# A chunk's query tokens by one DMA transpose of 512 rows instead of four of 128, with the projection reading whole rows

## The chip, the core and the metric

The kernel runs on one core of a Trainium2 chip. The metric is device time in microseconds (us): several runs of the kernel before and of the other kernel on the same chip. The record marks the state of each run, fast or slow; all runs that are compared by time here were fast. The profile is of one execution, recorded instruction by instruction. Engines are named as in the profile: PE is TensorE's matmuls, PEld its weight loads, DVE VectorE, ACT ScalarE, POOL GpSimd, and SPq the queue on which SyncE issues DMAs.

## The reference

One block of a Conformer over 2 batches of 4000 tokens with 512 features, in bfloat16. Cut to what matters here:

```python
x1 = x + 0.5 * (silu(ln(x) @ w_ff1_a) @ w_ff1_b)
h = ln(x1)
q, k, v = h @ w_q, h @ w_k, h @ w_v
scores = jnp.einsum('btd,bsd->bts', q, k) * D ** -0.5        # 4000 x 4000 per batch
x2 = x1 + jnp.einsum('bts,bsd->btd', softmax(scores), v) @ w_o
# ... then a convolution module, a second feed-forward part and a LayerNorm
```

## The kernel before

Tokens are worked on in chunks of 508 (four tiles of 127), eight per batch, the last of them with 444. The kernel folds `w_q` and `w_k` into one matrix `M`, so a query projection is `M` applied to the normalised tokens `h`, and the keys are `h` itself. During the first feed-forward part the normalised tokens are written to DRAM (`keysd`); attention fetches them from there, with the features on the partitions, by DMA transposes.

Where a chunk's query tokens land: a slot of 4096 bytes per partition, as four tiles, each with four contraction blocks of 128 tokens. The order in a partition's row is (tile, contraction block, token).

```python
oLT = take(2 * 4096)
self.lnT = [C.view(oLT + s * 4096, 2048).rearrange("p (t c k) -> p t c k", t=TPC, c=DC)
            for s in range(2)]
self.b_lnT = [[C.buf("lnT%d" % s, oLT + s * 4096 + j * 1024, 1024) for j in range(TPC)]
              for s in range(2)]
...
self.sT = C.view(oLT + 6144, 1024)...      # transposed row sums, in the second half of slot 1
```

The fetch, one call for each tile (127 or 111 query tokens, fetched as 128 rows), and the projection of one output block of 128 features:

```python
def fetch_queries(self, b, qc, ti):
    sl = self.query_slot(b, qc)
    src, rd = self.keys_at(b, self.query_at(qc, ti)[0])        # 128 rows of keysd
    self.transpose(self.lnT[sl][:, ti], src, rd, [self.b_lnT[sl][ti]])

def q_group(self, b, qc, dc):
    s, sl = qc % 2, self.query_slot(b, qc)
    ps, b_ps = self.sbank()
    W = width(qc)                                               # 508 or 444
    out = ps[:, 0:W].rearrange("p (t k) -> p t k", t=TPC)
    lo = self.query_at(qc, 0)[1]
    for cc in range(DC):
        self.mm(out, self.M[:, cc, dc * 128:(dc + 1) * 128], self.lnT[sl][:, :, cc, lo:lo + W // TPC],
                cc == 0, cc == DC - 1, [self.b_M] + self.b_lnT[sl], b_ps)
    ...                                                         # ACT or DVE copies ps to qT
```

So each projection matmul reads four pieces of 127 tokens that lie 1024 bytes apart. In attention over chunk g the fetch for chunk g + 1 is asked for at key tiles 7 to 10 of 32, and its four blocks of projection stand at key tiles 14, 16, 18 and 20:

```python
if g + 1 < NCK and g != 1 and 7 <= kt < 7 + TPC:
    self.fetch_queries((g + 1) // TCB, (g + 1) % TCB, kt - 7)
```

All DMAs of this kind go out on SyncE's queue in program order. A scheduler written in the kernel keeps track of buffers and emits a semaphore wait before an instruction where one is needed.

## Time and profile before

| | kernel before |
|---|---|
| time, median of 3 runs | 2034.23 us (2033.78 to 2035.38) |
| span of the profiled run | 2030.5 us |
| PE busy | 2021.3 us |
| granted clock | 0.999 |
| query transposes | 64, to landing 2.7 us |

The busy time of PE is almost the whole span, and the chain of work that ended last is 99% PE: whatever does not lengthen or shorten the row of matmuls is not seen in the time. Matmuls of 508 columns are listed with a mean duration of some 370 ns although the next one starts after some 215 ns: they overlap. For their cost one must look at the distances of their starts, which this document takes from the start times in the trace; the timeline shows them rounded to 10 ns. The lines themselves are shown in the prediction.

### The profile page before, as it was taken

The numbers are of one execution on the slowest core, as the hardware profiler recorded it, in microseconds if no ns is written. First come the engines' busy times: TensorE is split into PE (matmuls) and PEld (weight loads), VectorE is DVE, ScalarE is ACT, GpSimd is POOL, SyncE is SP. The second block draws the span as 40 slices with busy tenths as digits, with TensorE's granted clock in tenths as the row PEclk, the third lists the DMA queues.
The fourth block names the chain that finished last, engine by engine and source line by source line (L and its number), as shares of the span: only waits on it lengthen the run. The fifth ranks groups of instructions, "written<-read, shape, count | busy, mean of one in ns | idle before, by whom it ended". The sixth has DMA issues, their size and how long they took to land.

```text
span 2030.5 us, 25096 instructions
## 1 busy us (share of the span) xinstructions
PE 2021.3 (100%) x9874; PEld 1026.5 (51%) x9874; DVE 1089.1 (54%) x2237; ACT 740.0 (36%) x1275; POOL 108.0 (5%) x235
## 2 busy tenths in 40 slices
PE   9999999999999999999999999999999999999998
PEld 5555555554444444445444444444455555555555
DVE  4234443335556667667766676667674543444433
ACT  3433333333333333333333333333345443443433
POOL 1000000000000000000000000000011000000000
PEclk9999999999999999999999999999999999999999
DMA  8122245421101111113521111111143111111111
GB/s 190 48 62 63 53 100 127 96 68 25 20 16 32 27 35 27 32 27 90 122 54 27 29 32 32 27 30 30 44 139 94 32 32 41 32 31 42 30 34 38
DMA packets 264644, 107.03 MB, mean 53 GB/s; under 512 B 204932, under 2 KB 264007, under 8 KB 264519
## 3 DMA queue, kind: packets, MB, share of 16 engines
q1 hardware_dynamic: 263841, 105.01, 21.7%
q8 instruction: 80, 1.31, 0.3%
q14 instruction: 45, 0.37, 0.1%
q10 hardware_dynamic: 678, 0.34, 0.1%
HBM read 35.81 MB, written 23.86 MB: 29 GB/s over the span
## 4 chain that ended last, share of the span: by engine, by line
PE 99%; DVE 0%; ACT 0%; DMA 0%; issue 0%; POOL 0%; DVEq 0%; ACTq 0%
PE s L521 56%; PE y L521 43%; DVE work L633 0%; DMA work<-work 0%; ACT work L571 0%; PE y L549 0%; POOL work L740 0%; PE y L536 0%; DVE work L1376 0%; DVE work L735 0%; DVE work L653 0%; DVE work L568 0%; DVE wff L1254 0%; ACT keys L571 0%; DVE wff L1141 0%
## 5 line engine op out<-in xcount | busy, mean ns | idle before, releaser
L571 ACT ACTIVATE work<-s 128x508 bf16<-128x508 f32 (+3 forms) x1044 | 613.8, 589 | 1197.8 <-PE s L521 1192.4
L521 PE MATMUL s<-work,wff 128*128 128x508 bf16 (+4 forms) x2640 | 628.3, 369 | 1.0 <-DMA work<-work 0.7
L521 PE MATMUL s<-work,keys 128*128 128x508 bf16 (+2 forms) x2240 | 505.8, 356 | 0.0
L521 PE MATMUL y<-wff,work 128*127 128x512 bf16 (+1 forms) x2000 | 501.4, 378 | 0.0
L521 PE MATMUL y<-work,keys 128*128 128x508 bf16 (+1 forms) x1984 | 495.1, 373 | 0.0
L971 DVE TENSOR_TENSOR work<-work 128x508 f32<-128x508 f32 (+1 forms) x480 | 324.3, 676 | 265.2 <-ACT work L571 262.5
L521 PEld LDWEIGHTS s<-work,wff 128*128 128x128 bf16 x2640 | 252.6, 98 | 277.1 <-issue 4.7
L521 PEld LDWEIGHTS y<-wff,work 128*127 128x127 bf16 x2000 | 274.4, 137 | 170.9
L521 PEld LDWEIGHTS s<-work,keys 128*128 128x128 bf16 (+1 forms) x2240 | 195.7, 97 | 228.9 <-ACT work L571 5.8
L521 PEld LDWEIGHTS y<-work,keys 128*128 128x128 bf16 x1984 | 192.1, 97 | 226.7 <-DVE work L568 0.5
L767 DVE SCALAR_TENSOR_TENSOR xt<-y,xt 127x512 bf16<-127x512 f32 x125 | 77.8, 684 | 364.2 <-PE y L521 364.2
L633 DVE BATCH_NORM_STATS2 work<-xt 127x6 f32<-127x512 bf16 x311 | 195.6, 679 | 4.7 <-DMA xt<-in_x_dram 4.6
L521 PE MATMUL s<-work 128*127 128x512 bf16 (+4 forms) x775 | 195.7, 377 | 1.2 <-DVE work L1372 1.2
L640 POOL TENSOR_TENSOR work<-work 127x4 f32<-127x4 f32 (+1 forms) x76 | 76.6, 1008 | 1127.8 <-DVE work L638 1127.8
L521 PEld LDWEIGHTS s<-work 128*127 128x127 bf16 (+2 forms) x775 | 94.3, 124 | 74.7 <-issue 3.0
L653 DVE TENSOR_SCALAR work<-xt,work 127x512 bf16<-127x512 bf16 x309 | 111.7, 408 | 27.6 <-POOL work L640 23.2
L767 DVE SCALAR_TENSOR_TENSOR xt<-s,xt 127x512 bf16<-127x512 f32 x55 | 38.1, 692 | 148.5 <-PE s L521 148.5
L571 ACT ACTIVATE wff<-s 128x508 f32<-128x508 f32 (+2 forms) x83 | 44.0, 531 | 64.2 <-PE s L521 64.1
L767 DVE SCALAR_TENSOR_TENSOR xt<-s,work,xt 127x512 bf16<-127x512 f32 x64 | 48.0, 750 | 31.0 <-PE s L521 30.5
L1152 DVE SCALAR_TENSOR_TENSOR wff<-wff,s 128x508 bf16<-128x508 f32 (+1 forms) x57 | 38.7, 679 | 42.0 <-PE s L521 41.9
L571 ACT ACTIVATE work<-keys,work 128x508 bf16<-128x508 bf16 (+1 forms) x68 | 52.2, 775 | 0.4 <-DVE work L1268 0.2
L1233 POOL COPY wff<-wff 128x1 bf16<-128x1 bf16 x56 | 10.5, 188 | 633.8 <-DVE wff L1152 631.0
(94 smaller groups left out, 439.9 us busy)
## 6 DMA issues: line engine op xcount, KB each, us to landing
keys<-keysd SPq DMA_DIRECT2D x62, 128.0 KB, 2.3
keysd<-work SPq DMA_DIRECT2D x14, 448.0 KB, 3.2
out_dram<-work SPq DMA_DIRECT2D x14, 448.0 KB, 3.2
dcvd<-wff SPq DMA_DIRECT2D x48, 127.0 KB, 1.8
keys<-dcvd SPq DMA_DIRECT2D x12, 508.0 KB, 4.8
xt<-in_x_dram SPq DMA_DIRECT2D x13, 448.0 KB, 4.7
wff<-in_w_ff_a_dram SPq DMA_DIRECT2D x15, 256.0 KB, 4.8
work<-work SPq DMA_TRANSPOSE x208, 2.5
```

Of the source, the lines that this page charges most:

```text
L521: self.S.op("PE", lambda e: e.matmul(out, lhsT, rhs, start=start, stop=stop, **kw), reads=reads, writes=[bank], inc=stop if inc is None el ...
L571: return self.S.op("ACT", lambda e: e.activation(out, in_, func, **kw), reads=reads, writes=writes)
L633: self.S.op("DVE", lambda e: e.bn_stats(self.st[sl][:, ti, 0:6], x), reads=[b_x], writes=[self.b_st[sl][ti]])
L640: S.op("POOL", lambda e: e.tensor_tensor(out=self.rs[sl][:, 0:n], in0=self.mv[sl][:, 0:n, 1], in1=self.neghalf[0:TILE, 0:n], op=ALU.pow), ...
L653: self.S.op("DVE", lambda e: e.tensor_scalar(out, x, self.mv[sl][:, ti, 0:1], self.rs[sl][:, ti:ti + 1], ALU.subtract, ALU.mult), reads=[b ...
L767: self.S.op("DVE", lambda e: e.scalar_tensor_tensor(out=self.XT[g][rows], in0=ps[rows], scalar=scalar, in1=self.XT[g][rows], op0=ALU.mult, ...
L971: S.op("DVE", lambda e, p=p: e.tensor_tensor(out=acc, in0=acc, in1=self.P[p][:, 0:W], op=ALU.add), reads=[self.b_P[p], self.b_acc[s]], wri ...
L1152: self.S.op("DVE", lambda e: e.scalar_tensor_tensor(out=out, in0=th, scalar=1.0, in1=ps[:, 0:W], op0=ALU.add, op1=ALU.mult), reads=[b_ps, ...
L1233: S.op("POOL", lambda e: e.tensor_copy(self.G[gs][:, jj, 0:1], self.G[gp][:, jj, CHUNK:CHUNK + 1]), reads=[self.b_G[gp][jj]], writes=[self ...
```

## The change

The intent is twofold: fewer and larger DMAs, and a projection whose moving operand is one contiguous row. A slot is now seen as (contraction block, token), with rows of 512 tokens (448 in the last chunk, where 4000 tokens end). One transpose fills it, at the moment at which the first of the four was asked for.

```diff
-        self.lin = C.view(oLT + 4096, 2048).rearrange("p (c k) -> p c k", c=DC)
+        self.lins = [[C.view(oLT + s * 4096, DC * n).rearrange("p (c k) -> p c k", c=DC) for s in range(2)]
+                     for n in (512, 448)]
+        self.lin = self.lins[0][1]
...                                          (keys_at takes the number of rows)
-        out = ps[:, 0:W].rearrange("p (t k) -> p t k", t=TPC)
-        lo = self.query_at(qc, 0)[1]
+        lin, lo = self.queries(qc, sl)
         for cc in range(DC):
-            self.mm(out, self.M[:, cc, dc * 128:(dc + 1) * 128], self.lnT[sl][:, :, cc, lo:lo + W // TPC],
+            self.mm(ps[:, 0:W], self.M[:, cc, dc * 128:(dc + 1) * 128], lin[:, cc, lo:lo + W],
                     cc == 0, cc == DC - 1, [self.b_M] + self.b_lnT[sl], b_ps)
...
+    def queries(self, qc, sl):
+        last = qc == TCB - 1
+        return self.lins[last][sl], T - width(qc) - (T - 448) if last else 0
 
     def fetch_queries(self, b, qc, ti):
+        if ti:
+            return
         sl = self.query_slot(b, qc)
-        src, rd = self.keys_at(b, self.query_at(qc, ti)[0])
-        self.transpose(self.lnT[sl][:, ti], src, rd, [self.b_lnT[sl][ti]])
+        lin, lo = self.queries(qc, sl)
+        n = lin.shape[-1]
+        src, rd = self.keys_at(b, qc * CHUNK - lo, n)
+        self.transpose(lin, src, rd, self.b_lnT[sl])
```

A part of the change that the diff does not show: with one DMA per chunk there is one semaphore to wait for in place of four.

More of the change, by code (lines that the diff above doesn't have):

```diff
@@ L757, in store_keys, with keys_at @@
                     [self.b_h2[TPC - 1]], [self.b_tailsd[b]])
-    def keys_at(self, b, t0):
-        t1 = t0 + 127
+    def keys_at(self, b, t0, n=128):
+        t1 = t0 + n - 1
         rd = self.b_keysd[b * TCB + t0 // CHUNK:b * TCB + t1 // CHUNK + 1]
-        return self.keysd[b, t0:t0 + 128, :], rd + ([self.b_keyst[b]] if t1 >= T - TAIL else [])
+        return self.keysd[b, t0:t0 + n, :], rd + ([self.b_keyst[b]] if t1 >= T - TAIL else [])
     def residual(self, ps, b_ps, g, scalar, b_scalar=(), rows=slice(0, TILE)):
@@ L888, in q_group @@
             self.act(self.qT[s][:, dc, 0:W], ps[:, 0:W], AF.Copy, [b_ps], [self.b_qT[s][dc]])
-    @staticmethod
-    def query_at(qc, ti):
-        n = width(qc) // TPC
-        lo = max(0, qc * CHUNK + 3 * n + 128 - T)
-        return qc * CHUNK + ti * n - lo, lo
+    def queries(self, qc, sl):
+        last = qc == TCB - 1
+        return self.lins[last][sl], T - width(qc) - (T - 448) if last else 0
     def fetch_queries(self, b, qc, ti):
+        if ti:
+            return
         sl = self.query_slot(b, qc)
-        src, rd = self.keys_at(b, self.query_at(qc, ti)[0])
-        self.transpose(self.lnT[sl][:, ti], src, rd, [self.b_lnT[sl][ti]])
+        lin, lo = self.queries(qc, sl)
+        n = lin.shape[-1]
+        src, rd = self.keys_at(b, qc * CHUNK - lo, n)
+        self.transpose(lin, src, rd, self.b_lnT[sl])
     def row_max(self, qc):
```

## The prediction

> **What bounds the kernel now.** I read the page of the kernel before in this order: busy times, the chain that ended last, the costliest groups, the DMA issues. Then the timeline of TensorE (PE) and of SyncE's DMA queue (SPq) at the places the change touches, because a difference this small is only visible there.
>
> ```profile
> span 2030.5 us, 25096 instructions
> PE 2021.3 (100%) x9874; PEld 1026.5 (51%) x9874; DVE 1089.1 (54%) x2237; ACT 740.0 (36%) x1275; POOL 108.0 (5%) x235
> ...
> PE 99%; DVE 0%; ACT 0%; DMA 0%; issue 0%; POOL 0%; DVEq 0%; ACTq 0%
> ...
> L521 PE MATMUL s<-work,wff 128*128 128x508 bf16 (+4 forms) x2640 | 628.3, 369 | 1.0 <-DMA work<-work 0.7
> ...
> work<-work SPq DMA_TRANSPOSE x208, 2.5
> ...
> work<-keysd SPq DMA_TRANSPOSE x64, 2.7
> ```
>
> PE is busy for 2021.3 of 2030.5 us, and 99% of the chain that ended last is PE. The matmul group above is the only one whose idle time names a DMA, 0.7 us in all, and that DMA is "work<-work", a LayerNorm's transpose. The transposes that this change touches are the last line, "work<-keysd", 64 of them (16 chunks of four, 128 rows each); no matmul of the profile is waiting for one. The time is therefore the sum of the spacings of the matmuls, and a change counts only if it takes out matmul spacing or puts in a PE wait.
>
> **What the skill says, and whether the trace agrees.**
> 1. The Trainium skill, "TensorE: Matmul & The Clock Gate", section "Back-to-back issue gap": a warm matmul of N columns follows the one before after about N/2.4 + 2.5 ns. That is 214.2 ns at 508 and 215.8 ns at 512. The page gives no cost for a moving operand that lies in pieces. Differences of consecutive start times in the trace: matmuls that read a 508-wide contiguous row of the exponentials (y<-work,keys) start 213.4 ns apart on average, those that read 512 contiguous 215.8. The query projection reads four pieces of 127, and its 508 columns take 215.9, so four times 127 pays like four times 128.
> 2. The Trainium skill, "DMA: Bandwidth & Descriptors", section "Rules for kernel authors": coalesce many small transfers, and issue early and wait late, so that the fixed cost overlaps compute. The kernel already does the second: see the spare times below. So the first can win only queue time.
> 3. The Trainium skill, "Perfetto Trace Analysis", section "Per-instruction lifecycle: what the profiler-reported window actually captures": the span of a DMA instruction on its queue holds the issue, not the movement of data. The trace agrees: a query transpose occupies the queue for 1.27 us (median) and lands 2.7 us after its issue. I use both.
>
> **The change, part by part.**
>
> *Query projection (PE).* Its matmuls, 16 chunks of 4 output blocks of 4 contractions, stay 256. Only the moving operand changes: rows of 512 contiguous tokens, of which 508 are read. Timeline of PE in an attention chunk, columns start and busy time:
>
> ```profile
> 1004.91 1.02 PE L521 MATMUL y<-work,keys 128*128 128x508 bf16 x4
> 1005.77 1.03 PE L521 MATMUL s<-work 128*128 128x508 bf16 x4
> 1006.63 1.02 PE L521 MATMUL s<-work,keys 128*128 128x508 bf16 x4
> 1007.49 1.02 PE L521 MATMUL y<-work,keys 128*128 128x508 bf16 x4
> 1008.35 1.02 PE L521 MATMUL s<-work,keys 128*128 128x508 bf16 x4
> ...
> 449.28 3.62 PE L521 MATMUL s<-work 128*128 128x508 bf16 x16
> 452.73 0.81 PE L521 MATMUL y<-wff,work 128*127 128x512 bf16 x3
> ```
>
> The second line is a projection block: its four matmuls take 1.03 us from first start to last end where the others take 1.02. The block of 16 starts at 449.28 and the next matmul at 452.73: 3.45 us / 16 = 215.6 ns. The contiguous 508 columns take between 213.4 (the y<-work,keys lines, whose rows start on multiples of 1024 bytes) and 215.4 (the s<-work,keys lines, whose rows lie 1016 bytes apart; there every second matmul takes 217 to 218 and the others 213 to 214, so I take a start 8 bytes off to cost some 4 ns). The new rows are 1024 bytes apart, so I choose 213.4. Seven chunks of each batch are full: 14 x 16 = 224 matmuls x (215.9 - 213.4) = 0.56 us saved; 0.1 us if 215.4 should hold. The last chunk of a batch has 444 columns, now four pieces of 111 at 189.3 ns. In the new layout it reads 444 out of rows of 448, from column 4 on, 8 bytes off: contiguous 444 takes 187 where aligned and 190 where every second row is off, so 32 x (190 - 189.3) = +0.02 us. Sum on the path: **-0.5 us**, of 2034.
>
> *The transposes (SPq).* Four issues are replaced by one. What a transpose of 512 x 512 costs is in the profile: the weights are loaded by such ones.
>
> ```profile
> L579 SPq DMA_TRANSPOSE keys<-in_w_q_dram x1: 2255/2255/2255, 24.3 to 24.3; - x1
> DMA to landing us min/median/max: 4.7/4.7/4.7
> ...
> 926.66 1.19 SPq L579 DMA_TRANSPOSE work<-keysd  x1
> ...
> 935.61 1.27 SPq L579 DMA_TRANSPOSE work<-keysd  x1
> ...
> 656.26 5.11 SPq L579 DMA_TRANSPOSE work<-keysd  x4
> ```
>
> It occupies the queue for 2.26 us and lands after 4.7 us. Four of 128 occupy it for 5.11 us and the last lands some 3.8 + 2.7 = 6.5 us after the first issue. Per chunk the queue gets 2.8 us back, 16 x 2.8 = 46 us in all. No PE time lies there, so its worth on the path is **0**. The bytes stay the same (4 x 128 KB; a few rows that were read twice drop out).
>
> *The moment of the fetch.* All four quarters are now asked for at key tile 7 instead of 7 to 10 (chunk 0: at block 12 of the last feed-forward chunk, not 12 to 15; chunk 2: at key tile 24). The projection starts at key tile 14, so data comes earlier, not later. Tightest case of before: the fourth quarter issued at 935.61 and the first projection of that chunk at 941.58 on PE. With 2.7 us to landing that leaves 3.3 us spare. After, the whole is issued near 926.7 and lands near 931.4: 10 us spare. Chunk 0: first issue at 439.37, first projection at 449.28; 439.4 + 4.7 = 444.1, 5 us spare.
>
> *Waits added.* The single transpose writes a whole slot, so it must wait for the users of all its parts. The second half of slot 1 also holds the transposed row sums. Their reduction on VectorE (DVE) ends at 651.43 + 1.22 = 652.65 in the chunk whose fetch starts at 656.26, so this wait is over 3.6 us before.
>
> ```profile
> 651.43 1.22 DVE L1071 TENSOR_REDUCE work<-work 127x4 f32<-127x1024 bf16 x1
> ```
>
> Added to the path: 0. ACT and DVE keep their evictions and their sizes.
>
> **Rivals.**
> - *The projection waits for its data.* One wait for a transpose of 512 rows in place of four staggered ones. For it: a long transpose has to land whole, and near 930 us the queue also carries the second batch's keys. Against: 5 to 10 us spare as worked out. If the landing doubled to 9.4 us, chunk 0 alone would be about at its limit (448.8 against 449.28). One stall of 2 us is +0.1%.
> - *The long transposes hold up others on the DMA rings* (the tail probabilities, which go out and back, and the keys of batch 2). For it: 512 KB in one piece. Against: those 512 KB went out within 5 us before as well, and the queue is quiet around most fetches. A delay of up to 2 us in 16 chunks would be +30 us if nothing hid it; but PE waits for none of these now. I give it 1 to 2%.
> - *The freed queue time shortens the kernel.* 46 us of SPq would be 2.3% if the queue bounded anything. The chain of waits shows DMA at 0% and the matmuls 0.7 us of DMA wait. So at most 0.7 us: within the noise.
> - *The pieces cost much more than I see.* Ruled out by the 215.6 ns above: the most there is to take is 256 x 2.5 ns.
>
> **Range and chances.** 2034.23 - 0.5 = 2033.7 us. The three runs of before spread over 1.6 us (2033.78 to 2035.38), three times the effect, so the range is run-to-run spread and not doubt of the mechanism: 2031.5 to 2036.0. Faster by over 2% would need 41 us out of a PE that has only 9.2 us idle and 256 matmuls x 216 ns = 55 us of work concerned: 1%. Slower by over 2% needs a stall of 2.5 us in every chunk: 1%. Within 2%: 98%.
>
> **What would show each step right or wrong.**
> - Right: the transposes appear as "work<-keysd" x16 with 4 to 5 us to landing and 2.0 to 2.4 us of queue each; the projection's starts are 213 to 214 ns apart in full chunks (four matmuls in 0.855 us, where 0.863 before) and about 190 in the last ones; the PE busy time and the span are 0.3 to 0.7 us lower; PE's idle time names no "work<-keysd".
> - Wrong: projection spacing stays at 216 (then pieces were not the cost; the time stays anyway); an idle time before "s<-work" with DMA "work<-keysd" as releaser, most likely at chunk 0 near 449 us or at chunk 8 near 941 us; or to-landing times of the other DMAs that grow and show as waits of PE.

## The result, and the profile after

| | before | after |
|---|---|---|
| time, median of 4 runs each, same chip | 2034.10 us (2033.78 to 2035.38) | 2033.05 us (2032.49 to 2033.22) |
| span of the profiled run | 2030.5 us | 2029.1 us |
| PE busy | 2021.3 us | 2020.9 us |

The ratio is 0.9993 with a 95% interval of 0.9976 to 1.001. Ratios here are the mean time of one kernel's fast runs over that of the other's of the same rounds, so not quite the ratio of the medians. The interval contains 1: by time alone the two kernels are the same. The predicted 2033.7 us and its range hold the result.

From the page of the changed kernel (the line numbers in the program are two higher than before):

```profile
span 2029.1 us, 25033 instructions
PE 2020.9 (100%) x9872; PEld 1026.7 (51%) x9874; DVE 1089.0 (54%) x2237; ACT 739.4 (36%) x1275; POOL 108.0 (5%) x235
...
PE 99%; DVE 0%; DMA 0%; ACT 0%; SPq 0%; issue 0%
...
L523 PE MATMUL s<-work,wff 128*128 128x508 bf16 (+4 forms) x2640 | 628.5, 369 | 0.7 <-DMA wff<-in_w_ff_a_dram 0.4
...
work<-keysd SPq DMA_TRANSPOSE x16, 4.5
```

The bound is where it was, and the 64 transposes are 16 that land after 4.5 us. (9872 matmuls in place of 9874: two records are missing, while all 9874 weight loads are there.) One thing in the fourth line was not foreseen: the 0.7 us for which PE had waited for "work<-work" is no longer the releaser named. What is named now is a weight load in the first microseconds.

The timeline of PE at the two places that the prediction shows:

```profile
1004.99 1.02 PE L523 MATMUL y<-work,keys 128*128 128x508 bf16 x4
1005.85 1.02 PE L523 MATMUL s<-work 128*128 128x508 bf16 x4
1006.70 1.02 PE L523 MATMUL s<-work,keys 128*128 128x508 bf16 x4
...
449.59 3.59 PE L523 MATMUL s<-work 128*128 128x508 bf16 x16
453.02 0.81 PE L523 MATMUL y<-wff,work 128*127 128x512 bf16 x3
```

The 16 matmuls of chunk 0 take 453.02 - 449.59 = 3.43 us, where it was 3.45. By the start times, a block of four takes 0.8569 us on average in full chunks (0.8635 before) and 0.7500 us in the last chunks (0.7570 before).

SyncE's queue at the place that was the tightest, and the queue time of all 16 transposes (minimum, median, maximum in ns):

```profile
926.76 1.91 SPq L581 DMA_TRANSPOSE work<-keysd  x1
...
L581 SPq DMA_TRANSPOSE work<-keysd x16: 1461/1988/2770, 439.7 to 1395.4; - x16
```

### Where the difference lies

To see where 1 us comes from in 2030, I set the two traces beside each other matmul run by matmul run, counted from the first matmul of each, and looked at how far the changed kernel is ahead or behind. Between 100 and 1400 us it gains steadily, at the projections alone, 0.39 us in all. Between 1400 and 1500 us it gains 0.88 us: 0.03 at the last four blocks of projection and 0.86 at a single place. At the start it had lost 0.31 us. From 1500 us on nothing changes until the last matmul: the sum is -0.97 us. The other 0.44 us by which the spans differ lie after the start of the last matmul, 6.29 us from the end before and 5.85 after.

The single place, in the kernel before and then in the changed one; first SyncE's queue, then PE:

```profile
1482.83 6.09 SPq L579 DMA_TRANSPOSE work<-work  x4
...
1488.79 0.91 PE L521 MATMUL y<-work,keys 128*128 128x444 bf16 x4
1490.40 1.89 PE L521 MATMUL s<-work,wff 128*128 128x508 bf16 x8 [0.69 <-DMA work<-work]
```

```profile
1482.72 5.14 SPq L581 DMA_TRANSPOSE work<-work  x4
...
1488.68 0.91 PE L523 MATMUL y<-work,keys 128*128 128x444 bf16 x4
1489.43 1.89 PE L523 MATMUL s<-work,wff 128*128 128x508 bf16 x8
```

These are the transposes of a LayerNorm in front of the convolution, in the last chunk of attention, where no query is fetched any more. Four of them took 6.09 us to issue before and 5.14 after, the last one landed later, and PE had to wait 0.69 us for it (0.86 us between starts, since two matmuls in a row otherwise overlap by some 0.16 us there). The change touches none of these instructions. What differs is seen in the DMA queues. In the kernel before, in the stretch from 1484 to 1486 us:

```profile
q8 instruction: 1, 0.02, 3.5%
...
work<-work SPq DMA_TRANSPOSE x2, 3.7
```

In the changed kernel the same stretch has no such packet, and the transposes land in 2.5 us:

```profile
work<-work SPq DMA_TRANSPOSE x2, 2.5
```

The queue "q8 instruction" brings instructions: 80 packets of 16 KB in the whole run. The Trainium skill, "Runtime: NRT & Kernel Launch", section "Instruction fetch mechanics", says that each engine's instructions are refilled in blocks of 16 KiB, 256 instructions, by a DMA queue of the sequencer, and that the cost is mostly hidden. PE's 9874 matmuls, as many weight loads and 187 waits are 19,935 instructions, or 78 blocks of 256, so these packets are PE's program to all appearance. The packet near 1484.75 us (start in the trace) lies inside the issue of the second transpose, which took 2.20 us where a short one takes 1.27. In the changed kernel it comes at 1490.41 us, when the four are out. It moved, I suppose, because PE's program has 14 wait instructions less by then. How far each packet moves is not explained by that: most packets between 1070 and 1440 us came 1.1 to 1.6 us later, about what 14 instructions take at 0.1 us each, but this one came 5.7 us later.

In the trace of the kernel before the two often go together: from 45 us on there are 328 transposes of 128 rows on the queue. 18 of them took over 1.7 us to issue, and in 15 of these 18 a packet of q8 began during the issue (or up to 0.1 us before it); of the other 310 it was so in 6. But going together is not yet a cause, so the experiments ask for it.

### The profile page after: what moved, and what is told of

It is laid out like the page before. It is cut to its first block, busy times and chain, and to the rows that moved or that the text cites. A ratio compares the mean times of both kernels' runs of the same rounds, so it can differ in the third digit from the quotient of the medians.

```text
span 2029.1 us, 25033 instructions
## 1 busy us (share of the span) xinstructions
PE 2020.9 (100%) x9872; PEld 1026.7 (51%) x9874; DVE 1089.0 (54%) x2237; ACT 739.4 (36%) x1275; POOL 108.0 (5%) x235
## 4 chain that ended last, share of the span: by engine, by line
PE 99%; DVE 0%; DMA 0%; ACT 0%; SPq 0%; issue 0%
PE s L523 56%; PE y L523 43%; DMA wff<-in_w_ff_a_dram 0%; SPq L585 0%; DVE work L635 0%; PE y L551 0%; ACT work L573 0%; DVE work L570 0%; DVE wff L1257 0%; ACT keys L573 0%; DVE wff L1144 0%; DVE work L737 0%; ACT xt L573 0%; PE y L538 0%; DVE work L846 0%
```

## The experiments

The theory: the change saves in two places that have nothing to do with each other. (1) The whole-row reads make 64 blocks of projection faster by 0.4 us in all. (2) The shorter PE program moves the instruction fetches, and one of them no longer falls into the transposes at 1483 us, which takes 0.86 us of waiting away. Rivals: the saved queue time took the wait away; the wait comes and goes by chance; the reads need the single transpose; not the pieces but the places of the pieces cost.

All kernels below gave a result that the comparison with the reference accepted, and all runs had a granted clock of 0.999 or 1.0. e5, e6 and e7 were run once each, so that their times are not compared. e1 to e8 ran on one chip, e9 on another. Their times differ by less than their spread, as was to be expected of effects of 0.4 to 0.9 us, so each verdict rests on the traces. This is the account for all of them, in us: how far a kernel is behind (+) or ahead (-) of the first trace of the kernel before, counted from the first matmul, by stretches.

| run | up to 100 us | 100 to 1400 | 1400 to 1500 | at the last matmul | idle before 1490 | block of 4, full / last |
|---|---|---|---|---|---|---|
| before | 0 | 0 | 0 | 0 | 0.69 | 0.8635 / 0.7570 |
| after | +0.31 | -0.39 | -0.88 | -0.97 | none | 0.8569 / 0.7500 |
| e1 layout only | +1.19 | -0.40 | -0.07 | +0.72 | 0.66 | 0.8571 / 0.7500 |
| e2 after, PE padded | +0.28 | -0.40 | +0.13 | 0.00 | 0.85 | 0.8569 / 0.7504 |
| e3 before again | +0.43 | 0.00 | +0.37 | +0.79 | 1.06 | 0.8635 / 0.7570 |
| e4 after again | +0.67 | -0.40 | -0.88 | -0.61 | none | 0.8567 / 0.7499 |
| e5 pieces of 127 | +0.24 | 0.00 | -0.85 | -0.62 | none | 0.8635 / 0.7562 |
| e6 pieces of 254 | +0.50 | -0.40 | -0.88 | -0.79 | none | 0.8569 / 0.7500 |
| e7 8 bytes off | +0.57 | -0.40 | -0.88 | -0.71 | none | 0.8568 / 0.7500 |
| e8 before, PE +34 waits | +0.56 | 0.00 | -0.31 | +0.24 | 0.38 | 0.8635 / 0.7570 |
| e9 before, PE +64 waits | +0.25 | 0.00 | -0.86 | -0.62 | none | 0.8635 / 0.7565 |

The first column shows why times say so little: the first 100 us, when the first weights and tokens arrive, differ by up to 1.2 us between executions, more than either effect. The kernel before itself (e3) is 0.43 us behind itself there. The stretch from the start of the last matmul to the end varies too, from 5.4 to 6.6 us over these traces. The other columns repeat to some hundredths, but for the length of the wait.

### e1: the layout without the single transpose

```diff
 against the changed kernel
     def fetch_queries(self, b, qc, ti):
-        if ti:
-            return
...
-        n = lin.shape[-1]
-        src, rd = self.keys_at(b, qc * CHUNK - lo, n)
-        self.transpose(lin, src, rd, self.b_lnT[sl])
+        r0, r1 = ti * 128, min(lin.shape[-1], ti * 128 + 128)
+        src, rd = self.keys_at(b, qc * CHUNK - lo + r0, r1 - r0)
+        self.transpose(lin[:, :, r0:r1], src, rd, [self.b_q[sl][ti]])    # four buffers of their own
```

> The new layout and the whole-row reads, but four transposes of 128 rows at their old moments, with four semaphores. Theory (the change saves in two places: whole-row reads, some 0.43 us over all projections; and 0.8 us at one place near 1489 us, where PE waited for a LayerNorm transpose whose issue an instruction fetch of PE had held up, the fetch having moved because PE has 14 wait instructions less): projection blocks 0.857 us instead of 0.8635, PE's wait of some 0.7 us for work<-work near 1489 us is still there because PE's instruction stream is as long as before, time 0.3 to 0.6 us under the kernel before. Rival 1 (the saved queue time removed that wait): the wait is there too, same time. Rival 2 (that wait comes and goes by chance): wait there or not. Rival 3 (the saving needs the single transpose as well as the layout): blocks stay at 0.8635.

Measured: 64 transposes again (2.7 us to landing), and the projection blocks are at 0.8571 us: the whole saving between 100 and 1400 us is there. PE's program has 187 waits, as before, and the wait is there too:

```profile
1483.59 6.06 SPq L587 DMA_TRANSPOSE work<-work  x4
...
1491.12 1.89 PE L529 MATMUL s<-work,wff 128*128 128x508 bf16 x8 [0.66 <-DMA work<-work]
```

So the reads do not need the single transpose, and the single transpose adds nothing to them. The time was 2034.39 us (median of 5) against 2034.29 us of the kernel before (9 runs), ratio 0.9999 (0.9986 to 1.0013). The expected 0.3 to 0.6 us less is not seen in it; the profiled run alone had lost 1.19 us at its start.

### e2: the changed kernel with PE's program as long as before

```diff
 against the changed kernel; PADS makes the count of PE's wait instructions follow that of the kernel before
         lin, lo = self.queries(qc, sl)
+        if dc == 0 and not self.any_score:
+            for k in range(PADS[b * TCB + qc]):
+                self.nc.tensor.wait_ge(self.S.sem[self.S.dsems[k]], 16)    # reached long ago
```

> The changed kernel plus waits on PE that are long satisfied, so that PE's program has as many wait instructions as the kernel before (187) at the same places. Theory (fetch of PE's instructions collides with the issue of the transposes): the 16 KB instruction packet falls again near 1484 us into the four work<-work transposes, one of them is issued in some 2.2 us instead of 1.27, PE waits some 0.7 us near 1489 us, time only 0.3 to 0.6 us under the kernel before. Rival 1 (saved queue time): no wait, time some 1.0 to 1.3 us under. Rival 2 (chance): either.

Measured: 187 waits, the packet at 1484.58 us, and

```profile
1482.68 6.25 SPq L584 DMA_TRANSPOSE work<-work  x4
...
1490.40 1.89 PE L526 MATMUL s<-work,wff 128*128 128x508 bf16 x8 [0.85 <-DMA work<-work]
```

One transpose was issued in 2.37 us, and the wait is back, with all of the freed queue time still free. The rival of the queue time falls. Time: 2034.53 us (5 runs), ratio 1.0001 (0.9988 to 1.0015).

### e3 and e4: both kernels once more

No edit; each kernel unchanged.

> The kernel before once more, as a control for its trace. Theory and rival 1: the wait of some 0.7 us near 1490 us with work<-work as releaser is there again, ratio 1.000. Rival 2 (chance): it can be absent.

> The changed kernel once more, as a control. Theory and rival 1: no wait near 1489 us, time 0.8 to 1.3 us under the kernel before, of which 0.43 us in the projections. Rival 2 (chance): the wait can be there, and the time then only some 0.4 us lower.

Measured: the kernel before waits again (packet at 1485.28 us), the changed one does not (packet at 1490.68 us):

```profile
1491.19 1.89 PE L521 MATMUL s<-work,wff 128*128 128x508 bf16 x8 [1.06 <-DMA work<-work]
...
1489.78 1.89 PE L523 MATMUL s<-work,wff 128*128 128x508 bf16 x8
```

Times: 2034.95 us (5 runs) for the kernel before, ratio 1.0001, and 2034.11 us (5 runs) for the changed one against 2034.29 us, ratio 0.9996 (0.9983 to 1.001). All four traces of programs with 187 waits on PE (before, e1, e2, e3) have the wait and all five of programs with 173 (after, e4, e5, e6, e7) do not. So the wait is a property of the program; its length, 0.7 to 1.1 us, differs from run to run. In these rounds the medians lie only 0.2 us apart, not the expected 0.8 to 1.3: the size of the gain in time is not settled to better than the spread, and the two sets of the kernel before, 9 runs and 5, differ by 0.66 us in the median themselves.

### e5 and e6: what a piece costs

```diff
 against the changed kernel; e5 with 4 pieces, e6 with 2
+            x = lin[:, cc, :].rearrange("p (t k) -> p t k", t=4)[:, :, 0:W // 4]
-            self.mm(ps[:, 0:W], ..., lin[:, cc, lo:lo + W],
+            self.mm(ps[:, 0:W].rearrange("p (t k) -> p t k", t=4), ..., x,
```

> One transpose as in the changed kernel, but the projection reads its row of 512 as four pieces of 127 with one column left out between them (444: four of 111 out of 112). Wrong result on purpose: the tokens are shifted. Theory (the pieces themselves cost, as if each had one column more): blocks of four matmuls 0.8635 us again, 0.757 us in the last chunk of a batch; saving between 100 and 1400 us gone. Rival (the place of the pieces in four separate 4 KB tiles costs, not the pieces): 0.857 and 0.750 us.

> The same with two pieces of 254 out of 256 (222 out of 224). Wrong result on purpose. It asks what a piece costs. If each piece costs one column more: 510 columns, 215.0 ns, a block 0.860 us (last 0.7533). If a piece is rounded up to an even number of columns: nothing, 0.857 (0.750). If it is rounded up to 16 columns: 0.8635 (0.757).

The 16 matmuls of chunk 0 and the next matmul, in e5 and then in e6 (3.46 us and 3.42 us from start to start):

```profile
449.52 3.62 PE L523 MATMUL s<-work 128*128 128x508 bf16 x16
452.98 0.81 PE L523 MATMUL y<-wff,work 128*127 128x512 bf16 x3
...
449.78 3.59 PE L523 MATMUL s<-work 128*128 128x508 bf16 x16
453.20 0.81 PE L523 MATMUL y<-wff,work 128*127 128x512 bf16 x3
```

Measured: four pieces of 127 inside one row cost what four in separate tiles did (0.8635 us), so the place is not it. Two pieces of 254 cost nothing (0.8569 us, as the contiguous row; in the last chunk 2 x 222 at 0.7500). Two pieces as such are free, then, and the odd length, as it looks, is not: 127 pays as 128, 111 as 112. A matmul of four pieces of 127 starts the next after 215.9 ns, like one of 512 columns (215.8). Of the three readings that e6 was built to separate, rounding up to an even number fits. The feed-forward matmuls of three pieces of 127 (381 columns) agree: in the trace of the kernel before they start 162.6 ns apart, where 384 columns would take 162.5 by the prediction's formula. Two things stay open. Four pieces of even length were not run, so the number of pieces and their oddness are not separated by an experiment. And in the projections of the kernel before, e5 and e6 the output view was cut into the same pieces as the moving operand, so whether an odd piece costs in reading or in writing is not shown. Both kernels shift the tokens of the queries; the comparison accepted them all the same, so it is no check of the queries. One run each (2033.51 and 2033.33 us), no interval.

### e7: rows that start 8 bytes off

```diff
 against the changed kernel
-        return self.lins[last][sl], T - width(qc) - (T - 448) if last else 0
+        return self.lins[last][sl], 4 if qc else 0
```

> The changed kernel with the rows of all chunks but the first of each batch fetched four tokens earlier and read from column 4, 8 bytes off. Right result. The prediction's step (a start 8 bytes off costs some 4 ns for every matmul): blocks of 0.871 us in full chunks. What the last chunk of the changed kernel suggests (only the first of a block of four is late, by 3 ns): 0.860 us, as 218, 214, 214, 214.

Measured: a block takes 0.8568 us, no more than aligned. Within it the distances are 216.4, 213.6, 213.6 and 213.2 ns, so something moves from one matmul to the next and nothing is lost in the sum. The expectation from the prediction (0.871) and the one from the last chunk (0.860) are both wrong. One run, 2033.86 us.

### e8 and e9: the kernel before, with only the fetch moved

```diff
 against the kernel before; e8 with < 6, e9 with < 11
         lo = self.query_at(qc, 0)[1]
+        if dc and not self.any_score and b * TCB + qc < 6:
+            for k in range(3):
+                self.nc.tensor.wait_ge(self.S.sem[self.S.dsems[k]], 16)
```

> The kernel before, with nothing of the change, plus 34 wait instructions on PE (all long satisfied) in the first six chunks of attention, so that the fetch of PE's instructions near 1484.7 us comes some 3.6 us earlier, into a stretch in which no DMA is being issued. Theory (fetch collides with issue): no issue of work<-work over 2 us near 1484, no PE wait near 1489, attention some 0.8 us shorter at that place than in the kernel before, projection blocks still 0.8635. Rivals (saved queue time; the new layout): the wait of 0.7 to 1.1 us stays.

Measured: a miss by half. The packet came at 1483.85 us, only 0.9 us earlier than in the kernel before, and fell into the first of the four transposes, which took 1.87 us. The wait was 0.38 us. The three packets before that one had moved by 2.3 to 2.7 us. Why this one moved less I do not know. Time: 2034.30 us (6 runs) against 2034.32 us (10 runs), ratio 1.0001 (0.9988 to 1.0013).

> As e8, with 64 waits in place of 34, in eleven chunks; e8 had moved the fetch by 1.0 us only, onto the first of the four transposes, and PE still waited 0.4 us. Theory: the fetch now comes near 1481 to 1482.5 us, before the four transposes (1482.8 to 1489), all of them are issued in 1.2 to 1.3 us, PE has no wait for work<-work and the place takes 0.8 us less than in the kernel before; the projection blocks stay at 0.8635 us. Rivals: the wait stays at 0.4 us or more. Time: 0.8 us less at most, and lost in the spread.

Measured: the packet came at 1482.48 us, ahead of the four, and the timeline shows

```profile
1483.07 5.16 SPq L579 DMA_TRANSPOSE work<-work  x4
...
1489.79 1.89 PE L521 MATMUL s<-work,wff 128*128 128x508 bf16 x8
```

No wait, and 0.86 us gained at that place, with four transposes per chunk, the old layout, and 64 instructions more. The projection blocks stay at 0.8635 us. This is effect (2) alone, as e1 is effect (1) alone. One reservation: e9 ran on another chip than e1 to e8, and no profile of the unpadded kernel before is known to come from that chip; that the wait would have been there is taken from the other traces. e2, which brings the wait back by adding waits alone, does not depend on it. Time: 2033.91 us (4 runs) against 2034.56 (7 runs), ratio 0.9998 (0.9981 to 1.0014).

No version beyond the changed kernel was worth a further run: it has both effects already. The four-piece reads of the feed-forward matmuls would be the next candidate by number, but their tiles come as transposes of 127 tokens in 128 rows, and I did not try to lay these side by side.

## Why the prediction was right

- **What bounds the kernel: right.** PE is 99% of the chain in both profiles, and both gains lie in its row of matmuls.
- **The direction and the order of size: right.** Predicted -0.5 us on the path from the projections. Measured in the traces: 56 full blocks x (0.8635 - 0.8569) = 0.37 us and 8 short ones x 0.0070 = 0.06 us, together 0.43 us; e1 and e2 repeat it. Of the prediction's own signs, the busy time of PE is lower by 0.4 us as forecast; the span, 1.4 us lower where 0.3 to 0.7 was forecast, carries effect (2) and the differences at both ends as well.
- **The term for full chunks was mis-sized**: the prediction said "so I choose 213.4"; the measured distance is 214.2 ns. That is what the formula gives at 508 columns that the prediction itself quotes from the Trainium skill, "TensorE: Matmul & The Clock Gate", section "Back-to-back issue gap", 214.2. The 213.4 ns of the y<-work,keys lines hold for these beside the s<-work,keys lines, which take more: over a pair of such blocks the mean distance is 214.6. A distance should be read over whole blocks with their neighbours. So 0.37 us instead of 0.56.
- **The term for the last chunk had the wrong sign**: "so 32 x (190 - 189.3) = +0.02 us" rests on the step "I take a start 8 bytes off to cost some 4 ns". The last chunk went from 189.3 to 187.5 ns, and e7 shows that a start 8 bytes off costs nothing in the sum. The two errors, 0.19 us too much and 0.08 us too little, partly cancel: that the sum of -0.5 us came so near to -0.43 is in part luck.
- **The queue time: right.** "so its worth on the path is **0**": e1 has none of it and all of (1), e2 has all of it and none of (2). The queue time of a 512-row transpose is 1.99 us in the median and it lands in 4.5 us, against 2.26 and 4.7 assumed; all query transposes together took 83.3 us of the queue before and 32.5 us after.
- **The moment of the fetch and the added wait: right.** No PE idle time names a query transpose in any of the traces of this layout. The fetch that was watched begins at 926.76 us, as reckoned.
- **What the prediction did not see** is effect (2), 0.86 us, twice the 0.43 us of effect (1). It had that wait in front of it, 0.7 us, called it "a LayerNorm's transpose", and let only the freed queue time touch it ("So at most 0.7 us"); e2 shows that the queue time did not. That the wait instructions which the change removes shift the fetches of PE's program was in none of its rivals.
- **The range was an easy one.** It was made from the spread of runs, 2031.5 to 2036.0 us, and no change at all would have fallen into it as well. That the measured time lies inside says nothing for the mechanism; the traces do, for effect (1).

## What to carry to other kernels

Give a matmul an even number of columns per piece: here pieces of 254 were free and pieces of 127 or 111 paid one column each, so a piece count times the 0.43 ns measured (1.7 ns for four) tells at once whether that is worth a layout. When two nearly equal times are to be explained, lay the traces beside each other from the first matmul on, and before a sub-microsecond gain is put down to the change, check with a program of the same length whether it came from where the instruction fetches fell.

## What the Trainium skill lacked or had wrong

- "TensorE: Matmul & The Clock Gate", "Back-to-back issue gap", has its formula for an isolated matmul and gives some 131 ns for 512 columns in a stream of weight loads and matmuls. Here, in such a stream, 512 columns take 215.8 ns and 508 contiguous ones 214.2: the formula fits, the 131 ns does not.
- The same page says nothing of operands in pieces, and no page that I found gives a number for them: four of 127 take 215.9 ns, two of 254 take 214.2, four of 111 take 189.3 and two of 222 take 187.5.
- "Runtime: NRT & Kernel Launch", "Instruction fetch mechanics", calls the crossing of a 16 KiB block mostly hidden. Here such a packet goes along with a DMA issue of another engine's queue that takes 1.9 to 2.6 us instead of 1.27, and with the packet ahead of them PE gains 0.86 us there (e9; adding waits alone brings the loss back in e2). No page that I found says that instruction fetches and the issue of DMAs meet.
- "DMA: Bandwidth & Descriptors" gives no time on the queue for transposes of these sizes: the query transposes took 1.27 us for 128 x 512 and 1.99 us for 512 x 512 elements of bfloat16 here (medians), with 2.7 and 4.5 us from issue to landing.
